# Scores of three batches as split fp32r products, with a shorter ring of weight loads and a new order of instructions

## The chip, the cores and the metric

The kernel runs on one core of one Trainium2 chip. The metric is the device time of one execution in microseconds (us). Before the change three runs took 867.69, 867.75 and 869.7 us; their median is 867.75 us. TensorE is PE in what follows (its weight loads are PEld), VectorE is DVE, ScalarE is ACT, GpSimd is POOL, and SP is the engine whose queue issues nearly all DMAs.

## The reference

Attention of 8 batches, 8 heads, 576 positions and head size 64, on keys and values that are means of 8 neighbouring positions (so 72 keys), and then a feed-forward layer on all 4608 tokens:

```
k_p = k.reshape(B, H, 72, 8, 64).mean(axis=3);  v_p likewise
scores = (q @ k_p^T) / 8
attn   = softmax(scores)                       # with 1e-9 in the sum
x      = (attn @ v_p), heads joined            # 4608 x 512
h      = x @ w_in                              # 512 -> 2048
out    = (h * clip(h + 3, 0, 6) / 6) @ w_out   # 2048 -> 512
```

All inputs and the output are fp32.

## The kernel before

The tokens are worked off in twelve blocks (one of 512, one of 256, ten of 384). The first four go through the feed-forward layer by plain products (`Step.h`, line 1048, and `Step.out`, line 1078). The last eight are taken in pairs, by `super_block`: four pairs, each with a first half (line 1319, 384 columns a matmul, 28 chunks of weights with 12 matmuls each) and a second half (`out_seven`, line 1401, 256 columns a matmul, 28 chunks with 18 matmuls each). Nearly every large product is made as three fp32r matmuls of high and low parts, as in line 1400.

The weights of the last four pairs come from DRAM in chunks of 512 KB. `chunk` (line 1208 issues the DMA) keeps a ring of `NSTREAM` = 7 places, four in one pool (`wsFalse`) and three in another (`wsTrue`).

Attention runs beside the feed-forward work, two blocks or more ahead. A tile is 128 tokens, in two groups of four heads. `Scores.product` (line 686) makes the scores of one group: two head pairs, and for each one fp32 matmul of 144 columns with q as the stationary operand (`qt`) and the placed keys as the moving one (`kbd`). A tile that spans two batches has one matmul for each batch. The compiler turns one fp32 matmul into two PE instructions, each with a weight load of its own; an fp32r matmul is one. Then come the row maximum (DVE, line 690), the exponential (ACT, line 695), the division (POOL or DVE, lines 722 and 728), a transpose on PE (line 792) with a split on ACT and DVE (lines 803 and 804), and the product with the values (`av`, line 862).

`prep_k` (lines 489 and 498) sums the raw keys on DVE and places them, scaled, into `kbds[b % 2]`, two fixed fp32 buffers that are zeroed once.

The order on each engine is written out by hand: `ORDER` has one list of numbers for each of PE, DVE, ACT, POOL and SP, and `put_in_order` makes each instruction follow the one before it in the list. So an instruction that waits holds up all that stand behind it on its engine.

Of the kernel before, what the change touches and what calls it, by code (L numbers as in the profile page):

```python
# [17 lines left out]
P = 128  # L18
# [9 lines left out]

SIDE = 12
# [10 lines left out]
CHUNK, NSTREAM, NFIRST, NC, NREL = 2, 7, 4, 3, 2  # L40
# [16 lines left out]
        97-98 118 99 108-110 119 94 91 120-121 111 102-105 112 122 113 123-124 114 230 115 125 116-117 95 126-129  # L57
        211 130-132 92 133-134 142 135-137 212 143 138-139 213-214 140-141 160-161 148-149 144-145 162 146 150 163
        151-153 166 154 164 147 169-170 165 231 167-168 155 172 156 187 190 232 157 233 158-159 184-185 188-189 173
        191 174 171 175 196-197 176-177 193-194 198 178-180 199 181 186 182 192 183 200 215 195 201 218 202-203 221  # L60
        204 219 224 205 208 225 222 226 206 227 207 228-229 220 234 209 235 216 236 217 237 254 243 255-256 238
        257-258 248 210 223 239 251 259-260 240 249-250 244 261 274 282 241 283 262 245 252 263 275 253 264-265 242
        284-286 276 279 268 280 269 287 270 281 303 271 288 272 304 289 305 294 309 273 306 290 310-311 291 312 307
        331 292 313 293 314 317-318 300 308 332 334 333 335 337 319 338 320 246 336 321 339-340 295 322 301 247 341
        362-363 342 296 302 326 357 323 365 324 358 366-369 327 364 343-345 325 346 266 370 328 351 347-348 371 359
        352 372 385-387 267 373 388-389 374 354 277 353 278 375 391-392 355 376 356 416 393-394 382 390 395 419 383
        396 384 417 400 377 409 420 401-402 378 422 379 403-404 410 423 405 411 406 424-427 297-299 407 428 418 441
        454-455 408 315 456-458 429 438 444 430 442 421 451 431-433 445-446 316 459 452 460-463 439 464-465 482 440
        349 483-484 453 485-489 443 490 466 329 491 330 479 492 350 493 360 473 476 380 361 467-468 480 381 397-399
        477 494 474-475 478 495 412 481 497 500 503 413-415 498-499 434 501 435-436 504 509 447 437 448 505 496 449  # L70
        502 450 510 530 544 469 511-512 531 470-471 536 521 506 537 472 515 513 545 516 532 514 533 546 562 522 517
        534-535 538-543 547 507 548 508 549 527 550-552 556 553 557 554 558-559 518 555 560 523 561 519-520 564 524
        565-566 528 567 525 578-580 526 581 568-569 529 582 575 583-586 570 587-588 576 600 577 601 589 571 602-605
        572 606 597 607 592 608-609 598 620-621 610-611 593 573 622 563 623 594 599 617-618 624-625 629-630 614
        631-632 643 633 644 574 634 590-591 615 645 616 646-648 637 651 619 652-653 595-596 666 654 640-642 655 638
        656 612 663 667 613 626-628 664 635 668 665 669-671 639 636 657 686 658 674-677 687 689 678 659 690 679
        691-692 688 693-694 680 695-699 681 700 672-673 660 682 661 715 662 716-718 705 649 719-722 650 723 737 706
        712 707-708 724 731 738 713 739-740 732 725-726 714 734 741 733 742 755 683 709 747 756 748-750 761 751 757
        735-736 758 762 752 701 759 710 702 763-766 760 769-770 684 771 780 772 685 773-776 781 783-786 777 787-788
        797 791 805 792-794 806 795 807-808 798 796 799 809 782 802 810 803 811 804 823 817 820 812-813 818 814-816  # L80
        703 824 821 825 822 838 826 819 835 827-828 711 829 836 841-843 704 830-832 844 833 845-846 727 847 728 848
        743 849 834 729 850-851 753 744 754 852 837 745 730 839-840 856 853 746 857 767-768 854-855 858-859 862
# [12 lines left out]
        1191 1150 1167-1168 1188 1151 1179 1192 1175 1169 1205 1170-1172 1193 1215 1194 1180 1216 1195 1132 1217
        1196 1181 1197-1198 1212-1213 1218 1199 1142 1200 1116 1214 1143 1237 1206-1207 1219-1223 1243 1133 1228
        1244 1229 1117 1230-1232 1234 1245 1233 1246 1235 1134 1247-1250 1118 1251 1144 1264-1265 1135 1266 1238
        1267-1270 1239 1252 1271 1253 1236 1254 1272-1273 1145 1240 1119 1274 1241 1165 1275 1258-1259 1242 1261
        1255 1262-1263 1260 1303 1176 1166 1256-1257 1177 1279 1282 1152 1178 1304-1306 1283-1284 1276 1153 1280
        1307-1308 1311 1277-1278 1317-1319 1201 1312-1313 1291 1154 1320 1155 1314 1202 1315 1281 1316 1288  # L100
        1321-1323 1285 1324 1208 1325-1326 1209 1203 1329-1330 1327 1210 1182 1211 1289 1331 1328 1204 1335 1183
        1332 1286 1309 1333 1310 1334 1184-1185 1337 1287 1338 1290 1224 1336 1292 1225 1339 1293 1226 1294
        1340-1341 1227 1295 1300 1342 1296 1346 1301 1347 1354-1358 1360 1371 1359 1297 1362 1298 1363 1361 1379
        1302 1372 1364-1365 1299 1380 1385 1397 1386 1381 1366 1343 1367 1387 1382 1344 1383-1384 1388-1389 1398
        1390 1405-1407 1348 1408 1411 1409 1351 1349 1345 1391 1410 1413 1422 1414 1350 1352 1423 1412 1353 1392
        1376 1393 1368 1373 1369 1436 1374 1377 1375 1415 1370 1437 1416 1399 1417 1448-1449 1418 1394 1378 1402
        1395 1403 1396 1419 1430 1400 1404 1427 1431 1428 1432-1433 1420 1429 1434 1453 1421 1435 1439-1440 1462
        1441-1442 1401 1424 1443-1444 1463 1456 1425 1445 1426 1457 1450-1451 1446 1454 1484 1455 1464 1485 1481
        1458-1459 1452 1486 1460 1487-1488 1461 1478-1479 1465 1489 1466-1467 1482 1468 1438 1490 1494 1469-1470
        1480 1507 1495 1483 1496 1447 1471 1508 1497-1499 1472-1473 1500-1501 1513-1514 1510 1502 1515-1517 1511  # L110
        1518 1523-1526 1509 1512 1532 1538-1539 1527 1540 1528 1535 1541 1536 1542-1545 1529 1559 1546 1491 1537
        1556 1547 1530 1560-1563 1557 1548 1533 1564 1549 1531 1565 1534 1566-1567 1553 1568-1569 1558 1554-1555
        1580-1584 1570 1492 1503 1574 1585 1577 1493 1550 1586 1504 1587 1601-1604 1578 1474 1575 1579 1588
        1551-1552 1589-1590 1505 1605 1591 1571 1506 1572 1475 1576 1606-1608 1476 1573 1598 1477 1609 1622 1595
# [231 lines left out]
def attention_moe_kernel(  # L346
# [63 lines left out]
    def ring(name):  # L410
        return pool.tile([P, S], F32, name=name, tag="ring", bufs=4)
# [61 lines left out]
    def load_k(b, p):  # L473
        kraw[b, p] = ring("kst")
        nc.sync.dma_start(kraw[b, p], k[b, p])

    ksum = {}

    def prep_k(b, p):

# [1233 lines left out]
```

## Time and profile before

| | us |
|---|---|
| median of three runs | 867.75 |
| the profiled execution | 867.65 |
| its span in the trace | 865.8 |
| PE busy in the span | 857.1 (99%) |
| DVE busy | 671.9 (78%) |
| ACT busy | 557.8 (64%) |
| POOL busy | 96.6 (11%) |
| HBM rate over the span | 235 GB/s |

The profiled execution lies 0.1 us under the median, and 1.85 us of it lie around the span. On PE a matmul's recorded duration runs from its start to its end, and neighbours overlap; what a matmul costs PE in a dense stretch is the step from its start, or from the start of its weight load, to the next one. The opening takes about the first 35 us; the four pairs of blocks begin at about 329 us.

### The profile page before, as it was taken

The page shows a single profiled execution, that of the slowest core. Times are in us where ns is not written, and L with a number is a line of the kernel's source. Part 1 is how long each engine was busy: PE and PEld are TensorE (multiplying, and loading weights), DVE is VectorE, ACT ScalarE, POOL GpSimd, SP SyncE. Part 2 cuts the span into 40 slices and gives each one's busy share as a digit, 9 for nine tenths or more (in the row PEclk, how much of TensorE's full clock was granted, in tenths as well). Part 3 has the DMA queues.
Part 4 walks back from the last instruction along what each step waited for, and adds up shares of the span by engine and source line. Part 5 has one row for each costly group of instructions (what it writes and reads, how often), then busy time and mean ns, then how long its engine had stood idle before and what let it go on. Part 6 is the DMA issues. An engine that isn't in the chain of part 4 may idle for free.

```text
span 865.8 us, 16054 instructions
## 1 busy us (share of the span) xinstructions
PE 857.1 (99%) x5556; PEld 814.4 (94%) x5556; DVE 671.9 (78%) x1313; ACT 557.8 (64%) x1483; POOL 96.6 (11%) x188
## 2 busy tenths in 40 slices
PE   8999999999999999999999999999999999999998
PEld 8878889989889898999999999999999999999998
DVE  7989568887877678897998688899777697276764
ACT  5999648586657457677755677756785745255443
POOL 6210002030202002101101011201120000000000
PEclk9999999999999999999999999999999999999999
DMA  9981126455387778987787987878855788877874
GB/s 332 380 284 49 50 62 218 126 154 147 121 274 253 225 245 262 363 294 247 227 295 259 348 285 231 273 245 277 269 207 195 236 279 273 290 243 257 263 260 137
DMA packets 118095, 204.21 MB, mean 236 GB/s; under 512 B 13568, under 2 KB 72192, under 8 KB 118016
## 3 DMA queue, kind: packets, MB, share of 16 engines
q1 hardware_dynamic: 117872, 203.20, 70.9%
q8 instruction: 44, 0.72, 0.4%
q14 instruction: 35, 0.29, 0.1%
q10 hardware_dynamic: 144, 0.00, 0.0%
HBM read 164.37 MB, written 38.80 MB: 235 GB/s over the span
## 4 chain that ended last, share of the span: by engine, by line
PE 93%; DVE 3%; ACT 2%; issue 1%; DMA 0%; POOL 0%; SPq 0%; DVEq 0%; ACTq 0%
PE psx L1401 27%; PE psx L1319 26%; PE psh L1048 15%; PE pso L1078 15%; PE psa L862 4%; PE psa L686 4%; PE psa L792 2%; ACT e L695 1%; DMA stage<-k_l 0%; PE psa L794 0%; DVE sm L706 0%; DVE vst L606 0%; DVE mx L690 0%; POOL stage L580 0%; ACT r L1284 0%
## 5 line engine op out<-in xcount | busy, mean ns | idle before, releaser
L1319 PE MATMUL psx<-x,wsFalse 128*128 128x384 f32 x768 | 159.2, 342 | 0.0
L1048 PE MATMUL psh<-xhi,w 128*128 128x384 f32 (+2 forms) x520 | 157.4, 346 | 0.1
L1401 PE MATMUL psx<-wsFalse,part 128*128 128x256 f32 x1152 | 153.9, 283 | 0.0
L1401 PEld LDWEIGHTS psx<-wsFalse,part 128*128 128x128 f32 x1152 | 144.8, 189 | 0.0
L1078 PE MATMUL pso<-w,ghi 128*128 128x512 f32 x384 | 139.9, 403 | 0.0
L1303 ACT CAST part<-g 128x768 fp32r<-128x768 f32 x112 | 93.3, 836 | 65.7 <-PE psx L1401 60.3
L1319 PEld LDWEIGHTS psx<-x,wsFalse 128*128 128x128 f32 x768 | 133.5, 188 | 1.2 <-ACT c L1298 0.2
L1304 DVE TENSOR_TENSOR part<-g,part 128x768 fp32r<-128x768 f32 x112 | 107.5, 964 | 28.2 <-ACT part L1303 27.4
L1319 PE MATMUL psx<-x,wsTrue 128*128 128x384 f32 x576 | 124.8, 341 | 0.5 <-ACT c L1298 0.5
L1401 PE MATMUL psx<-wsTrue,part 128*128 128x256 f32 x864 | 117.1, 284 | 0.0
L1401 PEld LDWEIGHTS psx<-wsTrue,part 128*128 128x128 f32 x864 | 110.2, 191 | 0.0
L1048 PEld LDWEIGHTS psh<-xhi,w 128*128 128x128 f32 x520 | 94.9, 188 | 11.4 <-DVE g L1060 1.4
L1319 PEld LDWEIGHTS psx<-x,wsTrue 128*128 128x128 f32 x576 | 100.6, 188 | 1.2 <-ACT c L1298 1.1
L695 ACT ACTIVATE e<-psa,mx 128x72 f32<-128x72 f32 x256 | 80.3, 325 | 16.6 <-DVE mx L690 11.4
L1048 PE MATMUL psh<-xlo,w 128*128 128x384 f32 (+2 forms) x260 | 85.9, 342 | 0.0
L1298 ACT COPY c<-psx 128x384 f32<-128x384 f32 x96 | 45.8, 481 | 54.3 <-PE psx L1319 51.8
L1290 DVE TENSOR_TENSOR g<-psx,c 128x384 f32<-128x384 f32 x96 | 52.4, 555 | 36.6 <-PE psx L1319 21.3
L1078 PEld LDWEIGHTS pso<-w,ghi 128*128 128x128 f32 x384 | 70.9, 188 | 9.2 <-ACT ghi L1064 0.3
L1078 PE MATMUL pso<-w,glo 128*128 128x512 f32 x192 | 74.8, 400 | 0.0
L722 POOL TENSOR_TENSOR a<-e,sm 128x256 f32<-128x256 f32 x60 | 42.9, 716 | 239.9 <-DVE sm L711 188.8
L1284 ACT ACTIVATE r<-g,small 128x384 f32<-128x384 f32 x96 | 58.2, 618 | 15.5 <-DVE g L1290 12.6
L1285 DVE SCALAR_TENSOR_TENSOR g<-r,g 128x384 f32<-128x384 f32 x96 | 52.1, 558 | 11.7 <-ACT r L1284 11.4
(123 smaller groups left out, 1355.5 us busy)
## 6 DMA issues: line engine op xcount, KB each, us to landing
wsFalse<-wd SPq DMA_DIRECT2D x64, 512.0 KB, 4.9
wsTrue<-wd SPq DMA_DIRECT2D x48, 512.0 KB, 4.4
wsFalse<-w2t SPq DMA_DIRECT2D x40, 512.0 KB, 5.2
wsFalse<-w2d SPq DMA_DIRECT2D x24, 512.0 KB, 5.2
wsTrue<-w2d SPq DMA_DIRECT2D x24, 512.0 KB, 5.1
wsTrue<-w2t SPq DMA_DIRECT2D x24, 512.0 KB, 5.0
raw<-w_in_l SPq DMA_DIRECT2D x16, 512.0 KB, 9.3
raw<-w_out_l SPq DMA_DIRECT2D x16, 512.0 KB, 9.0
```

What stands on the lines that cost most here:

```text
L695: nc.scalar.activation(self.e[:, h], self.ps[:, h], AF.Exp, bias=self.mx[:, h : h + 1], **sums)
L722: engine.tensor_tensor(out=self.a[:, : 4 * D].rearrange("p (h s) -> p h s", h=4), in0=e[:, :, :D], in1=sm[:, :, None].broadcast_to([P, 4, D]),
L1048: nc.tensor.matmul(self.ps, l[f][:, c, :], r[:, c, :], start=c == 0 and i == 0, stop=c == NCC - 1 and i == 2)
L1078: nc.tensor.matmul(pos, l, r, start=f == 0 and i == 0, stop=f == NF - 1 and i == 2)
L1284: nc.scalar.activation(r, src, AF.Relu, bias=half_low, scale=GSCALE / (6.0 * WSCALE))
L1285: nc.vector.scalar_tensor_tensor(out=g_of[i][:, k], in0=r, scalar=GSCALE, in1=src, op0=ALU.min, op1=ALU.mult)
L1290: nc.vector.tensor_tensor(out=g_of[i][:, k], in0=ps, in1=kept, op=ALU.add)
L1298: nc.scalar.copy(c, ps)
L1303: nc.scalar.copy(t[:, 0], src)
L1304: nc.vector.tensor_tensor(out=t[:, 1], in0=src, in1=t[:, 0].bitcast(F32), op=ALU.subtract)
L1319: nc.tensor.matmul(ps, w[:, l, c * P : (c + 1) * P], t[:, r, c], start=o in (1, 2, 5) and c == 0 and k == 0, stop=c == 1 and k == 2, skip_ ...
L1401: nc.tensor.matmul(to, t[:, l, k, i * P : (i + 1) * P], w[:, k, r], start=begin and k == 0 and y == 0 and i % 2 == 0, stop=m == NM - 1 and ...
```

## The change

- For batches 5, 6 and 7 (`SPLIT_QK = 5`) the keys are placed as fp32r, and their low part (the scaled sum less the rounded key) goes to a second buffer, `klow`, by one DVE instruction for each half of a head pair.
- `split_q` makes, for each group of a tile, a high part of q (a cast on ACT) and a low part (a subtraction on DVE), 128 by 256 elements each. The buffer `q2` exists once; the second batch of a tile over two batches uses a place of the ring of small loads.
- `score_sums` gives for each head pair of these batches three fp32r matmuls of 144 columns (high q with high keys, high q with low keys, low q with high keys) in place of one fp32 matmul.
- The placed keys now come from a pool with two buffers, and each batch gets a new tile that POOL zeroes.
- `NSTREAM` goes from 7 to 6: four places in `wsFalse`, two in `wsTrue`.
- `ORDER` is another one on all five engines from about 35 us on; the opening stays as it was.

Counted over the program: 60 fp32 matmuls of line 686 (120 PE instructions) go, 180 fp32r matmuls come; DVE gets 30 subtractions of 128x256 and 24 instructions of 64x72 more, ACT 30 casts of 128x256, POOL 8 memsets of 128x576. The number of DMAs (585) stays.

```diff
+SPLIT_QK = 5
-CHUNK, NSTREAM, NFIRST, NC, NREL = 2, 7, 4, 3, 2
+CHUNK, NSTREAM, NFIRST, NC, NREL = 2, 6, 4, 3, 2
...
+    def keys_of(b):
+        if b not in kbds:
+            kbds[b] = pool.tile([P, NPAIR, 2 * SP], F32 if b < SPLIT_QK else F32R, name="kbd", bufs=2)
+            nc.gpsimd.memset(kbds[b].bitcast(F32), 0.0)
+        return kbds[b]
+
+    def low_keys(b):
+        if b % 2 not in klow:
+            klow[b % 2] = late[1].tile([P, NPAIR, 2 * SP], F32R, name=f"klo{b % 2}")
+            nc.gpsimd.memset(klow[b % 2].bitcast(F32), 0.0)
+        return klow[b % 2]
+
+    def split_q(tile, g):
+        for i, (b, _, _, _) in enumerate(tile):
+            if b < SPLIT_QK:
+                continue
+            if i and tile[0][0] >= SPLIT_QK:
+                x = ring("q2", F32R)[:, : NPAIR * P].rearrange("p (m c t) -> p m c t", m=2, c=2)
+            else:
+                x = late[1].tile([P, 2, 2, P], F32R, name="q2", bufs=1)
+            whole = qtiles[tile][i][:, 2 * g : 2 * g + 2]
+            nc.scalar.copy(x[:, 0], whole)
+            nc.vector.tensor_tensor(out=x[:, 1], in0=whole, in1=x[:, 0].bitcast(F32), op=ALU.subtract)
+            qparts[tile, i] = x
+
+    def score_sums(tile, p):
+        mms = []
+        for i, (qt, (b, _, _, _)) in enumerate(zip(qtiles[tile], tile)):
+            key = kbds[b][:, p]
+            if b < SPLIT_QK:
+                mms.append((qt[:, p], key))
+                continue
+            hi, lo = (qparts[tile, i][:, m, p % 2] for m in range(2))
+            mms += [(hi, key), (hi, klow[b % 2][:, p]), (lo, key)]
+        return mms
...
+                if b >= SPLIT_QK:
+                    nc.vector.scalar_tensor_tensor(
+                        out=low_keys(b)[at],
+                        in0=ks[rows],
+                        scalar=scale,
+                        in1=to.bitcast(F32),
+                        op0=ALU.mult,
+                        op1=ALU.subtract,
+                    )
...
-                for r, (qt, (b, _, _, _)) in enumerate(zip(qtiles[self.tile], self.tile)):
-                    nc.tensor.matmul(to, qt[:, p, :], kbds[b % 2][:, p, :], start=r == 0, stop=r == last)
+                mms = score_sums(self.tile, 2 * self.g + i)
+                for n, (l, r) in enumerate(mms):
+                    nc.tensor.matmul(to, l, r, start=n == 0, stop=n == len(mms) - 1)
...
     def scores(j, tile, g):
 
+        split_q(tile, g)
         s = Scores(tile, g)
```

In the lists that follow a row has its number in the engine's order, the line, and the operation with output and inputs; `x4` stands for four alike in a row. The changed file has other line numbers: 772 is the score matmul (686 before), 1406 and 1488 are the matmuls of the pairs (1319 and 1401), 540 and 541 are the two halves of `split_q`, 1295 is the load of a chunk (1208).

On PE, at the scores of the last tile that lies wholly in batch 6, before:

```order
2050 L862 MATMUL psa<-arem,vrem 128x384
2051 L1401 MATMUL psx<-wsFalse,part 128x256 x42
2052 L686 MATMUL psa<-kbd_83,qt 128x144 x4
2053 L1401 MATMUL psx<-wsFalse,part 128x256 x18
2054 L1401 MATMUL psx<-wsTrue,part 128x256 x36
2055 L792 MATMUL psa<-ident,a 128x128
```

The same tile after the change (its first group is `q_7750`, its second `q_7782`):

```order
2418 L772 MATMUL psa<-klo_6376,q_7750 128x144
2419 L1488 MATMUL psx<-wsFalse,part 128x256
2420 L1406 MATMUL psx<-x_7530,wsTrue 128x384
2421 L1406 MATMUL psx<-x_7452,wsTrue 128x384
2422 L772 MATMUL psa<-kbd,q_7750 128x144
2423 L1406 MATMUL psx<-x_7452,wsTrue 128x384
2424 L1488 MATMUL psx<-wsFalse,part 128x256
2425 L1406 MATMUL psx<-x_7530,wsTrue 128x384
2426 L1488 MATMUL psx<-wsFalse,part 128x256
2427 L1406 MATMUL psx<-x_7426,wsFalse 128x384
2428 L772 MATMUL psa<-kbd,q_7782 128x144
```

The four matmuls that stood together are twelve, one by one between longer ones; five matmuls of the pairs stand between the last product of the first group and the first of the second, which use the same `q2` buffer.

On ACT, at the same tile's casts, after the change:

```order
774 L1390 CAST part<-g_6547 128x768
775 L540 CAST q_7831<-qt 128x256
776 L1318 CAST x_7580<-x 128x768
777 L1385 COPY c<-psx 128x384
778 L576 ACTIVATE kbd<-ksum 64x72 x2
779 L540 CAST q_7782<-qt 128x256
780 L781 ACTIVATE e,sm<-psa,mx 128x72
781 L1385 COPY c<-psx 128x384
782 L781 ACTIVATE e,sm<-psa,mx 128x72 x2
783 L1318 CAST x_7687<-x 128x768
784 L540 CAST q_7828<-qt 128x256
```

The casts of q are new there; before, only the exponentials of a group (`e,sm`) stood on ACT between the copies and casts of the pairs.

On SP, at the first chunk loads, before:

```order
235 L1208 DMA wsTrue<-wd_96 128x1024
236 L1208 DMA wsTrue<-wd_97 128x1024
237 L1165 DMA wd_117<-wh 128x256
238 L1208 DMA wsTrue<-wd_98 128x1024
239 L1208 DMA wsFalse<-wd_99 128x1024
240 L1208 DMA wsFalse<-wd_100 128x1024
```

and after:

```order
237 L1295 DMA wsTrue<-wd_96 128x1024
238 L1171 DMA out<-o 128x512
239 L1295 DMA wsFalse<-wd_98 128x1024
240 L596 DMA vst<-v_l 128x2x256
241 L1295 DMA wsTrue<-wd_97 128x1024
242 L1295 DMA wsFalse<-wd_99 128x1024
```

Two of every six chunks, and no longer three of every seven, go to `wsTrue`.

## Rows read from the trace of the kernel before

**Rows 1.** The page: PE and PEld busy, the granted clock in 40 slices (9 is 90% or more of full speed), and the chain that ended last by engine.

```profile
PE 857.1 (99%) x5556; PEld 814.4 (94%) x5556; DVE 671.9 (78%) x1313; ACT 557.8 (64%) x1483; POOL 96.6 (11%) x188
PEclk9999999999999999999999999999999999999999
PE 93%; DVE 3%; ACT 2%; issue 1%; DMA 0%; POOL 0%; SPq 0%; DVEq 0%; ACTq 0%
```

**Rows 2.** Busy time by stretch: the stretch, its length, busy time of PE, PEld, DVE, ACT and POOL with the number of instructions, granted clock, DMA share, GB/s.

```profile
50.00:300.00 250.00, 249.64 (x1371) 220.27 (x1370) 194.10 (x438) 172.78 (x523) 27.01 (x55) 1.00 0.49 159
300.00:395.00 95.00, 94.51 (x525) 89.51 (x524) 79.09 (x161) 65.19 (x186) 11.01 (x18) 1.00 0.83 282
395.00:641.00 246.00, 245.65 (x1812) 244.12 (x1811) 205.99 (x405) 171.50 (x511) 34.18 (x60) 1.00 0.81 268
641.00:860.00 219.00, 219.00 (x1573) 218.21 (x1572) 149.20 (x225) 110.85 (x197) 1.73 (x4) 1.00 0.75 247
```

**Rows 3.** The score matmuls (line 686) from 394 to 642 us: count, duration in ns (least, median, most), first and last start.

```profile
L686 PE MATMUL psa<-kbd,qt x128: 283/286/362, 395.2 to 640.2; 128*128 128x144 f32 x128
```

**Rows 4.** The chain of waits, 600 to 645 us: start, us of the chain, what, instructions.

```profile
599.90 5.60 PE psx L1401 x47
...
611.64 1.47 PE psa L686 x12
...
619.01 1.40 PE psx L1319 x8
...
623.12 0.71 PE psa L862 x6
```

**Rows 5.** Timeline of the weight loads, 606.8 to 614 us: start, length, engine, line, shapes, count of like ones merged.

```profile
611.36 1.53 PEld L686 LDWEIGHTS psa<-kbd,qt 128*128 128x128 f32 x12
612.83 0.19 PEld L1319 LDWEIGHTS psx<-x,wsFalse 128*128 128x128 f32 x1
```

**Rows 6.** The same from 623.0 to 623.9 us: weight loads for matmuls of 192 columns in fp32r, one behind the other.

```profile
623.02 0.19 PEld L862 LDWEIGHTS psa<-ahi,vhi 128*128 128x128 f32 x1
623.12 0.19 PEld L862 LDWEIGHTS psa<-alo,vhi 128*128 128x128 f32 x1
623.23 0.19 PEld L862 LDWEIGHTS psa<-ahi,vlo 128*128 128x128 f32 x1
623.35 0.19 PEld L862 LDWEIGHTS psa<-arem,vrem 96*128 96x128 f32 x1
623.46 0.19 PEld L862 LDWEIGHTS psa<-ahi,vhi 128*128 128x128 f32 x1
623.57 0.30 PEld L1319 LDWEIGHTS psx<-x,wsTrue 128*128 128x128 f32 x2
```

**Rows 7.** The same from 109.7 to 110.6 us: the load behind an fp32 matmul of 64 columns, and the next.

```profile
110.08 0.19 PEld L1048 LDWEIGHTS psh<-xhi,w 128*128 128x128 f32 x1
110.19 0.43 PEld L862 LDWEIGHTS psa<-a,vrem 96*128 96x128 f32 x2
```

**Rows 8.** The same from 558 to 562.2 us: the loads of two transposes, of a third, and the next.

```profile
559.18 0.24 PEld L792 LDWEIGHTS psa<-ident,a 128*128 128x128 f32 x2
559.39 0.14 PEld L794 LDWEIGHTS psa<-ident,ar 128*128 128x128 f32 x1
```

**Rows 9.** Timeline of PE, 628.2 to 629.3 us: matmuls of 192 columns alone between matmuls of 384.

```profile
628.30 0.25 PE L862 MATMUL psa<-arem,vrem 96*128 96x192 f32 x1
628.38 0.36 PE L1319 MATMUL psx<-x,wsTrue 128*128 128x384 f32 x1
628.58 0.25 PE L862 MATMUL psa<-ahi,vhi 128*128 128x192 f32 x1
```

**Rows 10.** Instructions like those that are added or that the added ones wait behind: two of 394 to 642 us and one of 300 to 642 us (ns: least, median, most), two groups of the whole trace (busy us, mean ns, idle time before).

```profile
L803 ACT CAST ahi<-psa x31: 243/372/402, 402.0 to 640.0; 128x256 fp32r<-128x256 f32 x23, 128x128 fp32r<-128x128 f32 x8
L804 DVE TENSOR_TENSOR alo<-psa,ahi x31: 279/416/428, 406.3 to 641.4; 128x256 fp32r<-128x256 f32 x23, 128x128 fp32r<-128x128 f32 x8
L618 DVE SCALAR_TENSOR_TENSOR vlo<-vst,vhi x16: 252/286/291, 364.2 to 624.2; 64x128 fp32r<-64x128 f32 x16
L1303 ACT CAST part<-g 128x768 fp32r<-128x768 f32 x112 | 93.3, 836 | 65.7 <-PE psx L1401 60.3 <-DVE part L1304 2.5 <-DVE g L1285 1.1
L1094 POOL MEMSET kbd<- 128x576 f32 x2 | 1.1, 578 | 0.0
```

**Rows 11.** DMA issues of the chunks: count, KB each, median us from issue to landing.

```profile
wsFalse<-wd SPq DMA_DIRECT2D x64, 512.0 KB, 4.9
wsFalse<-w2t SPq DMA_DIRECT2D x40, 512.0 KB, 5.2
```

**Rows 12.** Waits of SP's queue: who waited for whom, us in total, times, longest.

```profile
SPq L1208 <- PE psx L1319: 160.2, 84, 6.3
SPq L1208 <- PE psx L1401: 143.7, 76, 6.8
```

More of the change, by code (lines that the diff above doesn't have):

```diff
@@ L61 @@
[L61 to L70, printed above, removed]
@@ new lines @@
+        1352 1397 1350 1353 1398 1405-1409 1391-1392 1373 1368 1393 1410 1369 1374 1376 1370 1422-1423 1377
+        1413-1415 1378 1375 1394 1436 1399-1400 1402 1416 1430 1395 1411 1396 1412 1431 1419 1417 1401 1420 1437
+        1432 1418 1433-1434 1421 1403 1462 1448 1404 1427 1438 1435 1439 1428 1424 1440 1429 1441 1453 1425
+        1442-1444 1463 1426 1464 1456 1449 1445 1450 1457 1451-1452 1484 1478 1454 1446 1485 1458-1459 1486
+        1460-1461 1455 1465 1487 1466 1488 1479 1489 1494 1467 1480 1468 1495 1481 1469-1470 1447 1496-1497 1471
@@ new lines @@
+        2055 2015 2056-2057 2016-2018 2059 2058 2060-2063 2039-2040 2026 2041-2043 2086-2090 2044 2091-2092
+        2071-2072 2064 2073 2093-2096 2074 2065 2075 2097 2076 2066-2069 2007 2070 2077 2008-2012 2110-2111
+        2098-2100 2112-2114 2046-2047 2078 2115 2101-2102 2048 2116 2049-2052 2083 2103 2084-2085 2117 2079
+        2118-2119 2080 2122 2081 2123 2082 2124-2125 2120-2121 2130-2132 2126-2127 2142 2133-2134 2128-2129 2143
+        2135-2136 2104 2137-2140 2144-2145 2141 2154 2146 2155 2105 2147 2166 2156 2187 2172 2157 2173-2174 2188
@@ new lines @@
+        2158 2175 2159-2160 2176 2167 2161 2177 2162 2178-2179 2106-2107 2180-2181 2189 2163 2190 2164 2182
+        2108-2109 2183-2186 2168 2193-2194 2165 2169 2195 2170 2191 2196-2197 2192 2198 2203-2206 2171 2148-2153
+        2221-2223 2209 2224 2210-2213 2207-2208 2265 2214 2266-2267 2215-2216 2231 2217 2232 2218 2199-2202
+        2219-2220 2233-2236 2243-2244 2225-2229 2268 2230 2237-2238 2245-2246 2239-2240 2259 2253 2241-2242 2287
+        2260 2288 2247-2248 2261 2313 2254-2255 2262-2264 2256 2269-2270 2249-2250 2257 2251 2314 2271 2334
@@ new lines @@
+        2272-2273 2252 2315 2258 2275-2279 2274 2281-2282 2280 2283 2295-2296 2284-2286 2297 2289-2291 2298
+        2292-2294 2335 2301-2302 2299 2303 2300 2304-2306 2316 2307-2311 2317 2312 2360 2322-2323 2361 2324
+        2318-2319 2325 2320 2326 2321 2338 2327 2339-2341 2344 2342 2328 2345 2329-2330 2362 2331 2336 2363 2332
+        2346-2351 2337 2352-2353 2333 2343 2354 2364 2355 2366-2367 2356 2368 2365 2357-2359 2369-2370 2378 2382
+        2371 2383 2372-2374 2384 2375-2377 2388 2385 2400-2401 2379 2389 2402 2386-2387 2390 2404 2391-2392
@@ new lines @@
+        2541 2549-2550 2542-2546 2572-2573 2551 2547 2554-2557 2574 2558 2552 2559 2553 2575 2560-2561 2584
+        2562-2563 2566 2564 2576 2567-2568 2577-2578 2569 2579 2570 2580 2585-2586 2565 2571 2581-2583 2587 2590
+        2588-2589 2591-2593 2602 2594-2595 2603-2604 2596-2600 2605-2606 2601 2607 2620-2621 2608-2609 2622
+        2610-2611 2623 2612-2613 2650 2614 2624-2625 2615-2619 2656 2626 2651 2627 2657 2628-2629 2652 2630-2632
+        2653 2668 2654 2633 2658 2634 2669 2638 2659 2645 2635-2636 2639 2692 2640 2660 2655 2661 2646 2693 2637
@@ new lines @@
+        2793 2781 2774 2782 2802 2799 2783-2784 2803 2800 2775 2794 2804 2785 2787 2786 2788-2789 2805 2790 2776
+        2791-2792 2806-2807 2777-2778 2808-2809 2779 2810-2812 2780 2819-2839 2846-2847 2813-2814 2848-2851
+        2815-2818 2852 2840-2845 2853-2908 2915 2925 2909 2919 2910-2913 2926 2914 2920-2921 2927 2922 2928 2953
+        2931-2932 2923 2937 2929 2933 2924 2930 2938 2959-2961 2954-2956 2941 2947-2948 2916-2917 2949 2942 2963
+        2943 2934 2944 2964 2918 2950-2951 2945 2939 2946 2952 2935 2965 2962 2966 2936 2969-2970 2967-2968
@@ new lines @@
+        4104-4105 4089 4106 4109-4110 4107-4108 4090 4050 4111 4051-4052 4115 4053-4055 4091 4116 4112 4117 4113
+        4118 4114 4092 4119 4068 4120-4121 4093 4122-4123 4069 4127 4124-4125 4128 4070 4126 4129 4133 4094 4134
+        4130 4135 4095-4096 4145-4147 4136-4138 4131 4139-4140 4132 4141-4142 4196 4143 4197 4148-4149 4144
+        4150-4152 4154 4198 4172 4153 4199 4173 4166 4155 4248 4156-4157 4184 4249 4185 4174 4167 4175-4177
+        4158-4162 4168 4178 4163-4164 4169 4179-4180 4165 4181 4186 4182 4300 4183 4301 4190 4170-4171 4191-4192
@@ new lines @@
+        4187-4188 4193 4189 4194-4195 4200-4201 4206 4202-4205 4212 4250 4213 4302 4214-4216 4303 4207 4251
+        4208-4209 4217 4210 4218 4211 4219 4224 4220-4221 4225 4222-4223 4230-4232 4226-4228 4233 4264 4252-4253
+        4229 4242-4243 4254 4234 4244 4255 4245 4265 4235-4239 4246 4240 4266 4256-4257 4241 4258-4259 4267 4260
+        4247 4261-4262 4268 4263 4270-4274 4269 4275-4279 4282 4280 4283-4285 4281 4286-4299 4304-4317 4322 4318
+        4323-4324 4340 4325 4319 4326 4320 4327-4328 4321 4329-4332 4341 4333-4338 4342-4345 4339 4346-4350
@@ new lines @@
+        5275 5270 5276-5277 5271-5272 5278 5273 5280-5284 5279 5285-5289 5292-5294 5290 5295-5297 5291 5298-5327
+        5334-5341 5328 5342-5343 5329-5333 5344 5346 5345 5347-5359 5364 5360-5361 5388-5389 5365-5366 5362 5400
+        5367 5363 5390 5370 5368-5369 5371 5401 5382 5391 5402 5392-5397 5372 5398-5399 5383 5373 5384-5385 5374
+        5386 5375 5406-5407 5376-5378 5408 5379-5380 5387 5403 5381 5404-5405 5409-5415 5418 5416 5419-5422 5417
+        5423-5430 5436-5438 5431-5435 5442-5453 5439-5441 5454-5459
@@ L314 @@
+        1169-1170 1173 1171-1172 1219 1174-1175 1178 1177 1176 1179-1180 1182 1181 1184 1183 1186 1185 1187 1189
+        1220 1190 1193 1188 1192 1191 1194 1198 1196-1197 1199 1201 1195 1200 1221 1202-1203 1206 1205 1204 1208
+        1207 1210 1209 1211 1213 1212 1214-1217 1222 1218 1223-1224 1226-1231 1225 1232-1234 1237-1240 1243
+        1235-1236 1241 1244-1245 1242 1246-1247 1249 1248 1250-1254
     """,
     "Pool": """
[L316 removed]
@@ new lines @@
+        394-395 392 407 397 403 396 404 411 398 412-413 400 408 406 410 401 409 417 414 418-419 415-416 420-421 423
+        422 424-427 429 428 430-431 445 433 432 446 438 434-435 439 449 437 436 451 440-441 447-448 444 442-443 452
+        454 450 459 453 455-456 458 461 457 462 466-467 463 468 460 464-465 469-474 477 475 478 476 481 479-480
+        482-485 487 486 488-489 491 490 492-495 498 496 499-504 497 505-514 516 518 515 519-520 517 521 524 522-523
+        525-559 562-566 560 567-568 561 569-576 579 578 580 577 581-582
@@ L408, in const, with ring @@
         return consts[f >= NF // 2]
-    def ring(name):
-        return pool.tile([P, S], F32, name=name, tag="ring", bufs=4)
+    def ring(name, dtype=F32):
+        return pool.tile([P, S], dtype, name=name, tag="ring", bufs=4)
     def behind(ins, name):
@@ L497, in prep_k @@
                 mul = nc.scalar.mul if b > 1 else nc.gpsimd.tensor_scalar_mul
-                mul(kbds[b % 2][rows, p - i : p + 1, h * SP : (h + 1) * SP], ks[rows], scale)
+                at = rows, slice(p - i, p + 1), slice(h * SP, (h + 1) * SP)
+                to = keys_of(b)[at]
+                mul(to, ks[rows], scale)
+                if b >= SPLIT_QK:
[7 more added lines that the diff above has]
+                    )
     vraw = {}
@@ L680, in product @@
             ps = att_bank()
-            last = len(self.tile) - 1
             for i in range(2):
-                p = 2 * self.g + i
                 to = ps[:, 2 * SP * i : 2 * SP * (i + 1)]
-                for r, (qt, (b, _, _, _)) in enumerate(zip(qtiles[self.tile], self.tile)):
-                    nc.tensor.matmul(to, qt[:, p, :], kbds[b % 2][:, p, :], start=r == 0, stop=r == last)
+                mms = score_sums(self.tile, 2 * self.g + i)
+                for n, (l, r) in enumerate(mms):
+                    nc.tensor.matmul(to, l, r, start=n == 0, stop=n == len(mms) - 1)
             self.ps = ps[:, : 4 * SP].rearrange("p (h s) -> p h s", s=SP)
@@ L1091, in attention_moe_kernel @@
     nc.gpsimd.memset(half, 0.5)
-    kbds = [fixed.tile([P, NPAIR, 2 * SP], F32, name=f"kbd{i}") for i in range(2)]
-    for t in kbds:
-        nc.gpsimd.memset(t, 0.0)
+    kbds = {}
+    for b in range(2):
+        keys_of(b)
     nc.scalar.activation(half, half, AF.Exp)
```

523 lines of the change are left out of this document (257 added, 266 removed), and 3 rows, old and new, of the table ORDER.

## The prediction

> **What bounds the kernel now.** I read the page first. PE is busy 99% of the span, its clock is granted in full in every slice, and the chain that ended last runs 93% over PE [rows 1]. Then the busy time by stretch: from 50 to 860 us, PE is busy 249.64 + 94.51 + 245.65 + 219.00 = 808.8 of 810 us [rows 2]. So behind the opening 1.2 us at most are waits; everything else is PE work, and what the change does to the time is what it does to PE's work, plus any wait that it brings in. A shorter time can come only from fewer or cheaper PE steps.
>
> The durations of matmuls don't tell their cost, since neighbours overlap: 286 ns for a score matmul [rows 3] is start to end. The cost is the step. In the chain, 8 matmuls of 384 columns take 1.40 us (0.175 each), 47 of 256 columns 5.60 us (0.119 each), 12 score instructions 1.47 us (0.1225 each) [rows 4]. The weight loads step in the same way: 12 loads for scores from 611.36 to 612.83 us, 0.1225 each [rows 5].
>
> **What goes.** 60 fp32 matmuls of line 686, two instructions each: 120 x 0.1225 = 14.7 us of PE. They all lie between 395 and 641 us, where 128 instructions of that line stand (the other 8 belong to batch 4) [rows 3].
>
> **What comes.** 180 fp32r matmuls of 144 columns, each with a weight load of its own. By columns alone they would be cheap: 0.175 us for 384 columns is 0.0656 for 144. But short matmuls don't step at that rate. Five of 192 columns stand one behind the other at 623 us, and their weight loads start at 623.12, 623.23, 623.35, 623.46 and the next at 623.57: 0.1125 each [rows 6], where columns alone would give 0.0875. In the chain six of them take 0.71 us, 0.118 each [rows 4]. Fewer columns don't help: behind a matmul of only 64 columns the load of 110.08 is followed by one at 110.19, 0.11 [rows 7]. The loads set the pace, and a load has 128 columns whatever the matmul has. Nor does it help that the new order puts these matmuls one by one between long ones. At 628.30 a matmul of 192 columns is followed after 0.08 us by one of 384, but that one then holds the next up until 628.58, 0.20 where 0.175 is usual [rows 9]: the sum is 0.28, as with 0.11 for the short one.
>
> Against this I weigh the Trainium skill. The page "TensorE: Matmul & The Clock Gate" gives, under "LDWEIGHTS (loading the stationary operand)", a load time of its columns over 1.2, which is 107 ns for 128 columns. By that rule the 180 matmuls would take an estimated 19.3 us and the time would come to 873.3 us, where columns alone would give 864.8; the steps of 0.11 to 0.1125 bear the rule out within 5%.
>
> The price has no row of its own, as no fp32r matmul of 144 columns is in the trace. From above: 0.118 each, the six in the chain, gives 21.2 us, so +6.5. From below: transposes load at 559.18 and, two later, at 559.39, 0.105 each [rows 8], which gives 18.9, so +4.2. I take 0.111, between the steps behind 64 and behind 192 columns, since 144 lies between: 180 x 0.111 = 20.0 us, **+5.3 us** on PE, all of it on the path.
>
> **Splitting q.** 30 casts on ACT at 0.372 us (like line 803, which casts as many elements) make 11.2 us; 30 subtractions on DVE at 0.416 (like line 804) and 24 low parts of keys at 0.286 (line 618) make 19.4 us; 8 memsets on POOL at 0.578 make 4.6 us [rows 10]. POOL's are hidden: it is busy 34 of 246 us where the scores lie. ACT goes there from 171.5 to 183 of 246 us. DVE goes from 206 to 225, that is 92% of the old length or 90% of the new [rows 2]: it stays under PE, but it is what becomes late next.
>
> What can reach PE is the buffer `q2`, which exists once. A group's cast must wait for the last product of the group before it, and the first product of the group waits for the cast. For the tile shown in the order, three matmuls of 384 and two of 256 stand between the two: 3 x 0.175 + 2 x 0.119 + the product's own 0.11 = 0.87 us. In that time the product must end (0.286) [rows 3] and the cast run (0.372): 0.66, and that only if ACT is free; a cast of line 1303 in hand takes 0.836 [rows 10]. Counted in the same way over the new order, ten of the thirty groups have less than 1.8 us. Nothing is lost if ACT is free each time; if each of the ten waits 0.6 it is 6 us. I take 0.1 each, **+1.0 us**, nearer to nothing because ACT is idle 30% of that stretch. Of what is queued behind a late cast, the exponentials and the copies of the pairs, none is nearer to PE than the score product itself.
>
> **The shorter ring.** A chunk feeds PE for 12 x 0.175 = 2.1 us or 18 x 0.119 = 2.14 us. With seven places a load starts six chunks before its use, 12.7 us; with six, five chunks, 10.6 us. It lands in 4.9 to 5.2 us [rows 11]. SP is early: it waits 304 us in all for places to come free, up to 6.8 at a time [rows 12]. So about 5.5 us of cover are left of 7.6, and I cost the ring at nothing, with up to 4 us if single loads are queued behind others.
>
> **The new order** can win at most the 1.2 us of waits that [rows 2] leave behind the opening, and can lose some: between -1 and +3, nothing taken.
>
> **Sum.** Against the profiled execution: 867.65 + 5.3 + 1.0 = 873.95 us; the median of the runs lies 0.1 higher, so **874.0 us**. This case alone reaches from 867.75 + 4.2 - 1 = 871 to 867.75 + 6.5 + 3 = 877.
>
> **Rivals.** *The products go at the column rate* (faster). If the weight load hides behind the neighbours, 180 x 0.0656 = 11.8 us, 2.9 less than before: 864.8 us. For it: the 0.08 us from a matmul of 192 columns to a long one [rows 9], no more than the 0.0875 that its columns need, and the many places where the new order puts them singly. Against it: the long one's 0.20, and the 0.1125 of [rows 6]. It decides when a product costs less than 14.7 / 180 = 0.082 us.
>
> *A product costs 0.08* (no change). If the recorded step behind a lone short matmul is its whole cost, 180 x 0.08 = 14.4, -0.3: 867.5 us. The 0.08 us of [rows 9] speak for it, the 0.20 of the long one behind it against. The skill's page named above has a second rule under "Back-to-back issue gap", about 81 ns a matmul at 128 columns in a stream with loads; by it the 180 products would take some 15 us and nothing would change. The steps in [rows 6, 7] are over a third above it, so I give this little.
>
> *The ring or the one `q2` runs dry* (slower still). A load that SP issues late because a load of q, keys or values stands before it in the queue lands after its use; four such at 1.5 us, beside the 6.3, give 880 us. For it: DVE at 90% and a ring with 2.1 us less cover. Against it: the cover that remains, and SP's waiting. It decides when a chunk's place is released over 5 us late.
>
> *The split is not made.* This is excluded by the order: 120 products with `kbd` and 60 with `klo` stand there.
>
> **Chances.** The forecast 0.75, the ring or `q2` 0.12, no change 0.08, column rate 0.05. About 0.3%, 2.6 us, can be told from no change here. So faster 0.05, within 0.3% 0.09 (the no-change case and the lowest corner of the forecast), slower 0.86. The range takes the forecast's own 871 to 877 and the third rival up to its price: 870.8 to 880.5; it leaves out the two cheap cases.
>
> **What would show it.** In the profile after: the score products of batches 5 to 7 as 180 instructions whose weight loads step by 0.108 to 0.118 us, with PEld near 1 in those stretches; line 686's successor using about 20 us instead of 14.7 there; PE busy still over 98%, and the last score later by about 5 us. Loads that step by 0.07 to 0.09 would prove the cheap rivals. Idle time before the products with ACT's line 540 as the releaser would size the 1.0 us; idle time before lines 1406 and 1488 ended by a DMA would mean the ring. The forecast is wrong if the time lies under 870 us, or if PE idles more than 4 us behind the opening.

## The result: 876.1 us, 1% slower

The changed kernel takes 876.08 us (median of 5 runs, 875.4 to 877.07), beside 867.75 for the kernel before (867.5 to 869.7): a ratio of 1.0092, 95% interval 1.0078 to 1.0106, so +8.3 us where +6.3 was forecast. The profiled run of the changed kernel took 875.4 us, its span 873.4: +7.6 against the span before.

### The profile after

The page, as in [rows 1]: busy time, granted clock, chain by engine.

```profile
PE 863.4 (99%) x5616; PEld 819.5 (94%) x5616; DVE 687.0 (79%) x1367; ACT 563.5 (65%) x1513; POOL 94.2 (11%) x196
PEclk9999999999999999999999999999999999999999
PE 89%; DVE 5%; DMA 2%; ACT 2%; issue 1%; SPq 0%; POOL 0%; ACTq 0%; DVEq 0%; POOLq 0%
```

The picture is the same: PE is full, its clock is granted in full, and there are 60 more instructions (180 for 120). The stretches of [rows 2], and the opening, with the same columns:

```profile
0.00:50.00 50.00, 44.62 (x260) 39.40 (x261) 41.52 (x83) 36.20 (x68) 23.13 (x52) 1.00 1.00 353
50.00:300.00 250.00, 249.57 (x1370) 219.62 (x1369) 196.72 (x444) 173.09 (x529) 27.19 (x58) 1.00 0.49 158
300.00:395.00 95.00, 95.00 (x528) 90.07 (x527) 76.79 (x160) 61.83 (x171) 11.06 (x18) 1.00 0.86 286
395.00:641.00 246.00, 244.93 (x1803) 242.71 (x1803) 206.88 (x418) 166.95 (x480) 25.79 (x54) 1.00 0.81 263
641.00:860.00 219.00, 218.95 (x1576) 217.54 (x1575) 159.27 (x257) 123.00 (x265) 7.00 (x15) 1.00 0.75 245
```

From 50 to 860 us PE is busy 808.5 us, where it was 808.8. In the first 50 it is busy 44.62, where it was 45.92 before: 1.3 us less, a loss that the forecast had not looked for. The 206.88 us of DVE and 166.95 of ACT from 395 to 641 us are not the 225 and 183 that the prediction adds up for that stretch, since part of this work now stands later. The score products now end at 688.7 us instead of 640 (row of line 772 in the instruction list):

```profile
L772 PE MATMUL psa<-kbd,q x120: 226/230/336, 398.6 to 688.7; 128*128 128x144 f32 x120
L772 PE MATMUL psa<-klo,q x60: 226/230/314, 407.1 to 688.6; 128*128 128x144 f32 x60
```

What a product costs is read from the weight loads. Timeline of PEld, 422 us (start, length, count of like ones merged): six products one behind the other.

```profile
422.26 0.19 PEld L772 LDWEIGHTS psa<-kbd,q 128*128 128x128 f32 x1 [0.32 <-ACT e L781]
422.37 0.19 PEld L772 LDWEIGHTS psa<-klo,q 128*128 128x128 f32 x1
422.48 0.30 PEld L772 LDWEIGHTS psa<-kbd,q 128*128 128x128 f32 x2
422.70 0.19 PEld L772 LDWEIGHTS psa<-klo,q 128*128 128x128 f32 x1
422.81 0.19 PEld L772 LDWEIGHTS psa<-kbd,q 128*128 128x128 f32 x1
422.93 0.19 PEld L949 LDWEIGHTS psa<-ahi,vhi 128*128 128x128 f32 x1
```

From 422.26 to 422.93 six steps, 0.112 each. And one alone among matmuls of 384 columns:

```profile
626.49 0.19 PEld L1406 LDWEIGHTS psx<-x,wsTrue 128*128 128x128 f32 x1
626.66 0.19 PEld L772 LDWEIGHTS psa<-kbd,q 128*128 128x128 f32 x1
626.83 0.19 PEld L1406 LDWEIGHTS psx<-x,wsTrue 128*128 128x128 f32 x1
626.94 0.36 PEld L1406 LDWEIGHTS psx<-x,wsFalse 128*128 128x128 f32 x2
627.29 0.14 PEld L879 LDWEIGHTS psa<-ident,a 128*128 128x128 f32 x1
```

From 626.49 to 627.29 stand four matmuls of 384 and the product: 0.80 - 4 x 0.175 = 0.10. A fit over all stretches of 25 PE instructions behind 125 us (their time against the number of each size in them, stretches with a wait left out) gives 0.107 to 0.110 for a product, 0.121 to 0.124 for an fp32 score instruction, 0.119 and 0.175 for 256 and 384 columns; how the stretches are cut moves it that much. With 0.110, 180 x 0.110 - 120 x 0.1225 = +5.1 us; with 0.107 it is +4.6.

The rest are waits. In the list of PEld's waits (who waited for whom, us in total, times, longest) all rows of 0.2 us and more add up to 13.6 us, 11.3 in the same list of before: +2.3. With 5.1 that is 7.4 of the 7.6 us of span. This is a rough account: a load can be late while a matmul still runs, and PE's own list grows by 1.4 only, from 5.1 to 6.5 us. Five of the rows that are new or have grown:

```profile
PEld psa L772 <- issue: 1.6, 1, 1.6
PEld psa L949 <- DVE vrem L719: 1.1, 2, 0.6
PEld psa L879 <- POOL a L808: 0.9, 2, 0.5
PEld psa L772 <- ACT e L781: 0.6, 2, 0.3
PEld psx L1406 <- DVE g L1377: 0.4, 2, 0.2
```

The largest is one place of the opening, PE at 36 us (in brackets: idle before, and what ended it):

```profile
36.36 0.48 PE L772 MATMUL psa<-kbd,qt 128*128 128x144 f32 x2 [1.39 <-DMA qt<-q_l]
```

Before, the load of this q (issued at 28.1 us, 8.4 to landing) was there at 36.5 and its scores stood at 37.67, so PE did not wait; in the trace of before:

```profile
L468 SPq DMA_DIRECT2D qt<-q_l x2: 546/546/546, 28.1 to 31.5; - x2
DMA to landing us min/median/max: 8.4/8.4/8.5
37.67 0.41 PE L686 MATMUL psa<-kbd,qt 128*128 128x144 f32 x2
```

The new order has them earlier. The second, 1.1 us behind `vrem`, lies at 207 us, in an earlier batch than those whose scores are split: that too is the order, on DVE. No row of PE or PEld names line 540, the cast of q.

### The profile page after: what moved, and what is told of

The parts are those of the page before. It is cut to its first block, busy times and chain, and to the rows that moved or that the text cites. A ratio compares the mean times of both kernels' runs of the same rounds, so it can differ in the third digit from the quotient of the medians.

```text
span 873.4 us, 16278 instructions
## 1 busy us (share of the span) xinstructions
PE 863.4 (99%) x5616; PEld 819.5 (94%) x5616; DVE 687.0 (79%) x1367; ACT 563.5 (65%) x1513; POOL 94.2 (11%) x196
## 4 chain that ended last, share of the span: by engine, by line
PE 89%; DVE 5%; DMA 2%; ACT 2%; issue 1%; SPq 0%; POOL 0%; ACTq 0%; DVEq 0%; POOLq 0%
PE psx L1406 27%; PE psx L1488 23%; PE pso L1165 15%; PE psh L1135 15%; PE psa L772 4%; PE psa L949 3%; PE psa L879 1%; DVE part L1391 1%; DMA qt<-q_l 1%; DMA stage<-v_l 1%; DMA wsTrue<-wd 1%; ACT e L781 1%; DVE g L1445 1%; PE psa L656 0%; DVE alo L891 0%
## 5 line engine op out<-in xcount | busy, mean ns | idle before, releaser
L1406 PE MATMUL psx<-x,wsFalse 128*128 128x384 f32 x912 | 197.6, 342 | 0.0
L1488 PE MATMUL psx<-wsFalse,part 128*128 128x256 f32 x1332 | 191.5, 283 | 0.1
L1488 PEld LDWEIGHTS psx<-wsFalse,part 128*128 128x128 f32 x1332 | 174.5, 189 | 0.9 <-DVE part L1391 0.8
L1406 PEld LDWEIGHTS psx<-x,wsFalse 128*128 128x128 f32 x912 | 159.1, 188 | 1.2 <-DVE g L1377 0.2
L1135 PE MATMUL psh<-xhi,w 128*128 128x384 f32 (+2 forms) x520 | 153.5, 345 | 0.0
L1406 PE MATMUL psx<-x,wsTrue 128*128 128x384 f32 x432 | 104.0, 344 | 0.2 <-DMA wsTrue<-wd 0.2
L1488 PE MATMUL psx<-wsTrue,part 128*128 128x256 f32 x684 | 103.3, 284 | 0.0
L1488 PEld LDWEIGHTS psx<-wsTrue,part 128*128 128x128 f32 x684 | 92.0, 190 | 0.0
L1406 PEld LDWEIGHTS psx<-x,wsTrue 128*128 128x128 f32 x432 | 76.0, 188 | 1.5 <-issue 0.4
L1371 ACT ACTIVATE r<-g,small 128x384 f32<-128x384 f32 x96 | 58.3, 619 | 14.7 <-DVE g L1377 13.6
L1143 ACT ACTIVATE g<-psh,small 128x384 f32<-128x384 f32 (+2 forms) x65 | 37.5, 577 | 38.5 <-PE psh L1135 31.8
```

What stands on the lines that cost most here:

```text
L1135: nc.tensor.matmul(self.ps, l[f][:, c, :], r[:, c, :], start=c == 0 and i == 0, stop=c == NCC - 1 and i == 2)
L1143: nc.scalar.activation(self.g, self.ps, AF.Relu, bias=half, scale=1.0 / (6.0 * WSCALE))
L1371: nc.scalar.activation(r, src, AF.Relu, bias=half_low, scale=GSCALE / (6.0 * WSCALE))
L1406: nc.tensor.matmul(ps, w[:, l, c * P : (c + 1) * P], t[:, r, c], start=o in (1, 2, 5) and c == 0 and k == 0, stop=c == 1 and k == 2, skip_ ...
L1488: nc.tensor.matmul(to, t[:, l, k, i * P : (i + 1) * P], w[:, k, r], start=begin and k == 0 and y == 0 and i % 2 == 0, stop=m == NM - 1 and ...
```

## Experiments

Each run was timed beside the kernel before on its chip (medians there 868.0 to 868.2 us, and 867.75 beside the changed kernel). So a difference from the 876.1 us of the changed kernel is one between chips, and taken from the kernel before on each it comes out 0.25 to 0.46 us larger.

**The products, undone.** e1 puts one fp32 matmul back for each three, and places the keys as fp32 for it:

```
-            mms += [(hi, key), (hi, klow[b % 2][:, p]), (lo, key)]
+            mms += [(qt[:, p], key), None, None]     # None: not issued
```

> The changed kernel, with the scores of batches 5 to 7 as one fp32 matmul each again, at the place of the first product of the three; the other two products are left out. The new orders, the ring of six and all the splitting on ACT, DVE and POOL stay, but nothing reads the parts. Theory (the products cost what their weight loads step by): 876.1 - 180 x 0.110 + 120 x 0.1225 = 871.0 us, and without the waits for `q2` (0.5 to 1) 870 to 870.7. Rival one (a product costs 0.08, so the three are worth no more than the fp32 matmul, and all of the loss is order, ring or splitting): 875 to 876. Rival two (the products run at the column rate, and the rest loses over 11 us): above 877.

The run took 871.02 us (870.66 to 871.83), a ratio of 1.0035 (1.0022 to 1.0048) to the kernel before. That is the theory's 871.0. So 5.1 us of the loss are the products and the waits that they bring, and 3 us are there without them. That a product is worth 0.08 is out.

**Columns or loads.** e2 gives the two products with a low part half their columns:

```
-                    nc.tensor.matmul(to, l, r, ...)
+                    w = SP if low[n] else 2 * SP
+                    nc.tensor.matmul(to[:, :w], l, r[:, :w], ...)
```

> The changed kernel, with the second and the third product of each three on 72 columns instead of 144, so that the second head's scores of batches 5 to 7 lack both low parts. Every weight load stays. Theory (the load sets the pace): nothing changes, 876.1 us, within 0.5. Rival (the columns do, at 0.175 us for 384): 120 x 72 x 0.000456 = 3.9 us less, 872.2.

The run took 875.07 us (874.87 to 875.67), 1.0 less where the theory allowed 0.5 and the columns would give 3.9. The loads of the six products of the same place, two threes of 144, 72 and 72 columns, in PEld's timeline of this kernel (the products are its line 777):

```profile
422.04 0.19 PEld L777 LDWEIGHTS psa<-kbd,q 128*128 128x128 f32 x1 [0.32 <-ACT e L788]
422.14 0.19 PEld L777 LDWEIGHTS psa<-klo,q 128*128 128x128 f32 x1
422.25 0.30 PEld L777 LDWEIGHTS psa<-kbd,q 128*128 128x128 f32 x2
422.48 0.19 PEld L777 LDWEIGHTS psa<-klo,q 128*128 128x128 f32 x1
422.59 0.19 PEld L777 LDWEIGHTS psa<-kbd,q 128*128 128x128 f32 x1
422.70 0.19 PEld L956 LDWEIGHTS psa<-ahi,vhi 128*128 128x128 f32 x1
```

That is 0.66 us for six, 0.11 each, with four of them at half the columns. The load sets the pace. Of the 1.0 us I know no place; the spans of the two profiled executions differ by 0.3 us only (873.4 and 873.1), and the two ranges overlap.

**One product fewer.** e3 leaves out the product with the low keys.

```
-            mms += [(hi, key), (hi, klow[b % 2][:, p]), (lo, key)]
+            mms += [(hi, key), None, (lo, key)]
```

> The changed kernel without the 60 products of q's high part with the low keys, so two products for each score of batches 5 to 7; all else stays. Theory (a product costs 0.110 wherever it stands): 60 x 0.110 = 6.6 us less, 869.5 us. Rival (column rate, 0.0656): 3.9 less, 872.2. Rival (0.08 each): 4.8 less, 871.3.

The run took 870.28 us (870.15 to 871.78): 5.8 less, 0.097 for each product left out. This lies between the theory's 0.110 and the 0.08 of the rival; by the trace the products that are left still step by 0.11 (the fit gives 0.111 to 0.114). What is missing came back as waits, as the last runs show.

**The waits for `q2`.** e4 takes q's parts out of the products, so that neither waits for the other:

```
-            hi, lo = (qparts[tile, i][:, m, p % 2] for m in range(2))
+            hi = lo = klow[b % 2][:, 0, :P]
```

> The changed kernel, with columns of the low keys in the place of q's parts as the stationary operand of all 180 products, so those scores hold nothing of q. PE runs as many instructions of the same size in the same order, the splitting is still done, but no product waits for a cast or a subtraction, and no cast waits for a product. Theory (waits for `q2` cost PE 0.5 to 1 us): 875.1 to 875.6 us. Rival (the one `q2` costs the whole remainder beside the products, 3 us): 873. Rival (nothing at all): 876.1.

The run took 875.66 us (875.16 to 875.98): 0.4 less, and its range overlaps with that of the changed kernel, so the waits cost between 0 and 1 us. The mechanism is there, but on ACT; waits of ACT in the changed kernel from 395 to 700 us:

```profile
ACT q L540 <- PE psa L772: 6.1, 9, 1.7
```

Nine of the thirty casts came too early for their buffer and stood 6.1 us in all, and PE hardly waited for one. In this run's list the row is gone.

**The opening.** e5 moves the scores behind the landing of their q (in PE's order):

```
-        211-212 129 213 130-135 92 214 142 136 ...
+        211 129-135 92 212-214 142 136 ...
```

> The changed kernel, with the three score matmuls of the second tile in the opening moved behind eight other matmuls, past the landing of their q at 36.2 us, for which PE stands still 1.4 us in the changed kernel. Theory (this wait is the one place where the new order costs a piece of its own): 876.1 - 1.3 = 874.8 us. Rival (what is moved ahead or comes behind then waits instead, since DMA sets the end of the opening): 876.1.

The run took 874.6 us (874.11 to 874.82): 1.5 less, as the theory has it. The place at 36 us is gone from the list; one of 0.36 us, for POOL's `kbd` at 43 us, is new, so a part of the wait moved on, as the rival has it.

**The order and the ring alone.** e6 leaves out all of the change's arithmetic: e1, and no cast of q, no low parts of q and keys, no memsets of `klow`. The new pool of placed keys stays, with its eight memsets of `kbd` on POOL where there were two. e7 is e6 with the edit of e5.

```
-            nc.scalar.copy(x[:, 0], whole)
-            nc.vector.tensor_tensor(out=x[:, 1], in0=whole, in1=x[:, 0].bitcast(F32), op=ALU.subtract)
...
-                    nc.vector.scalar_tensor_tensor(out=low_keys(b)[at], ...)
```

> The changed kernel without the change's arithmetic: one fp32 matmul for each score of batches 5 to 7 as before, no casts, subtractions, low keys or memsets. Only the new orders and the ring of six are left of the change. Theory (the splitting hides beside PE and the remainder of the loss is order and ring): as the run with fp32 scores, 870 to 871 us. Rival (the remainder is DVE and ACT being late because of the splitting): that of the kernel before, 868.

> The kernel with only the new orders and the ring of six left of the change (fp32 scores, no splitting), and the three score matmuls of the opening behind the landing of their q. Theory (order and ring cost 2 to 3 us, 1.3 of it there): 1.3 less than the same without the move, 869 to 869.5 us. Rival (the wait moves on): no less.

e6: 870.21 us (869.4 to 870.53), ratio 1.0025, 1.0016 to 1.0034. e7: 869.35 (868.87 to 869.87), 1.0016, 1.0008 to 1.0025. So the order and the ring, with the pool of placed keys, cost 2.2 us with nothing else of the change, 0.9 of it at 36 us; the wait for `vrem` at 207 us (1.0 us in two pieces) is in e7's list too. Which part of the last 1.35 us is the ring's was not tried: the order is written for its ring. The trace of the changed kernel has one wait of PE for a chunk, 0.2 us. Between e6 and e1 lie 0.8 us for the splitting, which PE does not read there; the intervals of the two ratios overlap, so this is at the edge of the noise. Two waits that go with it, in e1 and in the changed kernel and not in e6, PEld from 375 to 400 us in the changed kernel:

```profile
PEld psx L1406 <- DVE g L1372: 0.3, 1, 0.3
PEld psx L1406 <- DVE g L1377: 0.2, 1, 0.2
```

**One product alone.** e8 leaves 60 products:

```
-            mms += [(hi, key), (hi, klow[b % 2][:, p]), (lo, key)]
+            mms += [(hi, key), None, None]
```

> The changed kernel with only the product of the high parts for each score of batches 5 to 7, 60 products instead of 180, so these scores are as coarse as the high parts; the splitting is still done. Theory (0.110 each, wherever it stands): 876.1 - 120 x 0.110 = 862.9 us, and more if DVE, with less time under PE, becomes late: up to 865. Rival (0.097 each, as the run without the products with the low keys came out): 864.5. Rival (column rate, 0.0656): 868.2.

The run took 867.3 us (867.11 to 868.54): only 8.8 less, outside what the theory allowed, 0.073 for each of 120 products, and nearest to the column rate's 868.2. Either a product is cheaper than its loads say, or the time comes back. e9 takes DVE's splitting out as well; e10 adds the edit of e5 to it. Edit of e9 over e8, the memsets with it:

```
-            nc.vector.tensor_tensor(out=x[:, 1], in0=whole, in1=x[:, 0].bitcast(F32), op=ALU.subtract)
...
-                    nc.vector.scalar_tensor_tensor(out=low_keys(b)[at], ...)
```

> The run with one product for each score of batches 5 to 7, 867.3 us, and now also without the subtractions and the low keys on DVE and the memsets of the low keys; the cast of q stays, and the scores are as coarse as its high parts. That run gave back 8.8 us for 120 products, where 0.110 each would be 13.2. Theory (the missing 4.4 us are PE waiting for DVE, which has the same 19 us of splitting to do in less time): 863 to 864.5. Rival one (they are waits that the order sets, whatever DVE has to do): 867. Rival two (a product costs PE only 0.073): 867.

> The same, and the three score matmuls of the opening behind the landing of their q, worth 1.5 us in the changed kernel and 0.9 with fp32 scores: 0.9 to 1.5 less than the run beside it. It is the candidate that could beat both kernels, at the price of coarser scores: 862 to 863.5 us by the theory (DVE), 866 by the rivals.

e9: 866.25 us (865.67 to 866.55), 1.05 less than e8, where the theory of a late DVE asked for 2.8 to 4.3. It falls: DVE's extra work is about a quarter of it. The two rivals, waits and a cheap product, have the same price here, so the time does not tell them apart and the traces must. PEld's waits from 395 to 700 us, first in the changed kernel, then in e9 (its lines are 14 higher):

```profile
PEld psx L1488 <- DVE part L1391: 0.8, 3, 0.3
PEld psa L772 <- ACT e L781: 0.6, 2, 0.3
PEld psa L879 <- POOL a L808: 0.5, 1, 0.5
...
PEld psx L1406 <- DVE g L1377: 0.2, 1, 0.2
```

```profile
PEld psx L1420 <- DVE g L1391: 1.4, 5, 0.4
PEld psa L786 <- ACT e L795: 1.4, 2, 0.8
PEld psa L893 <- POOL a L822: 1.3, 4, 0.5
PEld psx L1502 <- DVE part L1405: 0.8, 3, 0.3
```

All rows of 0.2 us and more add up to 3.2 us in the changed kernel and to 7.2 in e9. The spans differ by 873.4 - 864.3 = 9.1 us; 120 x 0.110 = 13.2, less 4.0 of new waits, is 9.2. That sum rests on the load's waits, and PE's own list grows by less (0.8 to 2.0 us). But both kernels run all other matmuls in the same order, so a product's price can be read place by place. One place in the changed kernel, then the same in e9:

```profile
500.31 0.34 PE L1406 MATMUL psx<-x,wsTrue 128*128 128x384 f32 x1
500.49 0.23 PE L772 MATMUL psa<-klo,q 128*128 128x144 f32 x1
500.55 0.56 PE L1406 MATMUL psx<-x,wsTrue 128*128 128x384 f32 x2
500.95 0.51 PE L1406 MATMUL psx<-x,wsFalse 128*128 128x384 f32 x2
```

```profile
498.18 0.69 PE L1420 MATMUL psx<-x,wsTrue 128*128 128x384 f32 x3
498.71 0.52 PE L1420 MATMUL psx<-x,wsFalse 128*128 128x384 f32 x2
```

Three matmuls of 384 columns and the product take 0.64 us, the three alone 0.53: 0.11, though only 0.06 lie between the product's start and the next one's. Over the 38 places where e9 leaves out a product that stood alone, and none right behind it, the time from the matmul before it to the second one behind it is shorter by 0.112 us in the median, and the first of these two intervals by only 0.066, the column rate; in e3 the same two are 0.112 and 0.066 at 19 places. So a product costs PE 0.11, alone or not, and a third of what its removal frees is lost again as waits. The longest are for the chains score, `e`, `a` and transpose, and `g` to the next matmul. That these take as long as before, so that in an order made for three products PE now arrives early, fits the list but was not tried. e10: 865.61 us (865.24 to 866.26), ratio 0.9971, 0.9958 to 0.9983, which is 0.6 less than e9 where 0.9 to 1.5 was expected: faster than both kernels by a little, but with scores of batches 5 to 7 from the high parts of q and keys alone, which is another computation than the fp32 one.

## Why the prediction was right, and where it was not

- **Products, +5.3.** This was right, in the size and in the mechanism. e1 and the changed kernel differ by 5.1 us with the waits for `q2` in it, the steps give 4.6 to 5.1, and 0.111 was taken where 0.107 to 0.112 came out. Long neighbours hide nothing (0.112 for a lone product), so the "column rate" is out, and so is 0.08. The reading of [rows 9], that the matmul behind a short one pays the rest, holds too. The Trainium skill's load time ("TensorE: Matmul & The Clock Gate", "LDWEIGHTS (loading the stationary operand)"), 107 ns for 128 columns by that page, is within 3% of the trace's 0.110. The same page's 81 ns ("Back-to-back issue gap") is not met here.
- **`q2`, +1.0.** This was probably too high: it is 0.4 by e4, and between 0 and 1. ACT had the slack, as the forecast said it might; nine casts waited, where it counted ten close places, and the waits fell on ACT.
- **Splitting hidden beside PE.** It was not wholly hidden: 0.8 us (e6 to e1, at the edge of the noise), of which 0.5 can be seen as PE's weight loads waiting for `g` of DVE. DVE was named as what becomes late next, with no price.
- **The ring, 0.** Nothing in the trace speaks against it: 0.2 us of waiting for a chunk. It was not tried by itself. The third rival's price, four waits of 1.5 us, rests on no row, and no wait of that size for a chunk came.
- **The new order, 0 (-1 to +3).** This is the term that was mis-sized: 2.2 us (e6) with the ring and the pool of placed keys in it, inside the +3 that was allowed for. The step that failed is "can win at most the 1.2 us of waits that [rows 2] leave behind the opening, and can lose some ... nothing taken". It looked behind the first 50 us, where there was little to win, and not at the opening itself, where two rows of the order against the landing of one load would have shown the 1.4 us.
- **Sum.** 5.1 (e1, with `q2`) + 0.8 + 2.2 = 8.1 for the measured 8.3, and 6.3 was forecast; the 0.25 that is left lies between the two measurements of the kernel before. The time came out inside the forecast's own 871 to 877 because of the 3 us allowed for the order. Three sums of the working are off: the upper end of 877 leaves out the 1.0 for `q2`, the 864.8 and 867.5 us of the cheap cases do too, while the 873.3 beside them has it, and a step of 0.1125 is 5.5% above 107 ns and not within 5%. None of them changes which way the time was to move. Of the signs, the loads' step, PE's busy share and PE's idle time held. The last score does not lie 5 us later but 48: the order spreads the products to 688 us, and the forecast had not followed it that far.

## What to carry to other kernels

Price a short matmul by the step of its weight load, measured at places like the one where it will stand; its columns, its start-to-end time and the step from it to the next matmul all mislead. When an order is written anew, hold each moved instruction against the landing time of what it needs, in the opening too: one row cost more here than all the waits for the single buffer. And work taken from the engine that sets the end comes back in part: of 13.2 us taken, 9 were kept.

## What had not been expected of the hardware

- An fp32r matmul of 72 columns behind its own weight load takes the same 0.11 us as one of 144, 0.66 us for six.
- A lone product of 144 columns lengthens the interval in which it stands by 0.066 us only and the next one by the rest; over both it costs 0.112.
- An fp32 score instruction (two for each matmul) steps by 0.121 to 0.124 at 144 columns, an fp32r one by 0.107 to 0.112: splitting in three can't win at this size, whatever hides the casts, since 3 x 0.110 is more than 2 x 0.1225 (e1, with one fp32 matmul in place of the three, took 5.1 us less).
